# The band of softmax weights by column group, its zeroing on VectorE, and one scaling that may start three units sooner

## The chip, the cores and the metric

The kernel runs on one core of one Trainium2 chip. The metric is the time of one execution on the device in microseconds (us); of several runs the median is given. The engines are TensorE (PE in the profile, its weight loads PEld), VectorE (DVE), ScalarE (ACT), GpSimd (POOL) and SyncE (SP). SP and POOL issue nearly all DMAs here.

## The reference

Two branches work on the same input x of 2048 tokens by 1024. Branch a is an attention with 32 heads of 32 channels in which each token sees eight tokens: itself and those 2, 4, ... 14 before it. Branch b is a gated feed-forward layer with 3584 hidden channels. A sigmoid gate per token mixes the two.

```python
x = A_x
g = _sigmoid((x * gate_w).sum(-1, keepdims=True))
a = _A_ref(x, A_wqkv, A_wo)      # q, k, v; softmax over 8 keys at distance 0, 2, .. 14; times v; times wo
b = _B_ref(x, B_w_gate, B_w_up, B_w_down)   # (gelu(x @ w_gate) * (x @ w_up)) @ w_down
return g * a + (1 - g) * b
```

Inputs and result are bf16.

## The kernel before, in words

The big matrix products use a Strassen-like scheme of seven products in place of eight, so every group of weights and of activations is first combined by additions on VectorE. The tokens are worked on in two halves, s = 0 and 1, of 1024.

**Units.** The first 70% of the time is a list of units (class `Unit`, line 372). A unit is 28 products of 128x512 (line 381), about 6.05 us of TensorE, and goes through `p1`, `p5` and `p26`, while the unit before it finishes with `p73` and `p4`. TensorE's order per unit is: p1 of this unit, p73 of the one before, p5, the attention's slots, p26, and p4 of the one before. ScalarE copies partial sums between PSUM banks and evacuates them (lines 398, 403, 386 or 388, 410). VectorE adds two banks at once in line 417; the product of p4 overwrites one of these banks, so TensorE waits for line 417 there. The units are first one pair of the feed-forward layer, then q and k for both halves, then v, then the rest of gate and up. For the q and k units the weights are read with a step of eight columns (line 482).

**Background work on VectorE.** Everything else that VectorE does is a task: a generator that records some instructions and then yields their estimated cost in us. `bg(gen, prio, wake)` (line 448) puts a task in a list ordered by priority, the smallest first, and `wake` is the first unit in which it may run. At the end of each unit's recording `run_bg` (line 456) takes steps from the first awake task until a credit of some 4.7 us is used up. Each engine executes its instructions in the order in which they were recorded. So a task that is awake earlier, or has another cost, moves all others.

**The attention's second half.** The softmax weights of every head are written to DRAM (`w_d`, line 728). For each window of 114 tokens (`BQ`) and each half the kernel builds a band matrix: for 128 keys by 114 tokens by 32 heads, with the eight weights of a token on their diagonals and zero elsewhere. Its steps are these, and `pv_plan` (line 797) gives each a unit counted from the unit b in which the last softmax tasks allow it:

- `pv_init` (line 738, unit b): zeroes three band buffers `band` of 128 x 3648 bf16 and two staging tiles `ct` of 128 x 480, and stores the zeros to three DRAM copies `b_d`. All of it is on POOL.
- `pv_weights` (line 746, units b+2 and b+13): SP loads the weights from `w_d`.
- `pv_turn` (line 751): TensorE transposes two tiles of 128x128 (line 756), ScalarE copies them into `ct` (line 759), POOL writes `ct` into `b_d` with a row step that puts each weight on its diagonal (line 762).
- `pv_fetch` (line 764): two units later SP loads the nonzero parts of the band in three pieces (line 770), and the 128 rows of v (line 773).
- `pv_mm` (line 777): three units after that, 16 products per half of the heads (line 783). Each has a stationary operand of 32 columns of v and a moving operand of one head's band, 114 columns. The four heads c = 0 to 3 go to four groups of 32 output partitions, so that four products run beside each other. ScalarE evacuates them (line 786).

The band lies as [token][head], so the columns of one head's band are 32 elements, or 64 bytes, apart in SBUF.

**The results of gate and up** are multiplied by line 262, multiplied by 1 - g where they are among the last pairs (line 265), and stored to `h_d` by POOL (line 268). The tiles that hold them form a ring of five (`st_tile`, line 232).

**The end.** `run_last` and `down` (line 1107) multiply the hidden channels by w_down and the attention by wo, in one product whose left operand is loaded back from `h_d` and `o_d`. Those loaded blocks that were not multiplied by 1 - g before are scaled on VectorE by `scale_task` (line 950, its instruction is line 955). `pre_down_0` (line 990) loads the first eleven blocks of the operand A21 ten units before the end (n is the number of units) and makes a task of priority 6 of their scaling; it may run from unit n - 2. The other scalings have priorities 3, 7 and 8.

Of the kernel before, what the change touches and what calls it, by code (L numbers as in the profile page):

```python
# [10 lines left out]
BF16 = mybir.dt.bfloat16  # L11
F32 = mybir.dt.float32
AX = mybir.AxisListType
AP = bass.AP

P = 128
SC = 512
SUP = 2 * SC
NWIN = 8
DIL = 2  # L20
HALO = 16
AC = 256
NJ = 4
# [29 lines left out]
BQ = 114  # L53
BK = BQ + HALO - DIL
NSUB = 3
SQ = BQ // NSUB
R_BAND = (32, 39.125, 46.25)
# [3 lines left out]
R_CT = (72, 90)  # L61
# [7 lines left out]
def _win_ap(src: bass.AP, dims):  # L69
    return AP(src.tensor, src.offset, [list(src.ap[0])] + [list(d) for d in dims])  # L70
# [3 lines left out]
def kernel(  # L74
# [12 lines left out]
    nc = tc.nc  # L87
# [7 lines left out]
    NT = KT  # L95
# [12 lines left out]
    def reg(kb, n):  # L108
        o = int(kb * KB)
        return arena[:, o:o + n]  # L110

    def reg3(kb, a, b):
        return reg(kb, a * b).rearrange("p (a b) -> p a b", a=a)

    def reg4(kb, a, b, c):
        return reg(kb, a * b * c).rearrange("p (a b c) -> p a b c", a=a, b=b)
# [6 lines left out]
    def bank(i):  # L123
        return banks[:, i, :]
# [12 lines left out]
    PW = HALO + SUP + HALO  # L137
    w_d = [tc.dram_tile([32, NWIN, PW], BF16, name=f"w_d{s}") for s in range(2)]
    BC = BQ + 2 * (HALO - DIL)
    b_d = [tc.dram_tile([BK, BC, 32], BF16, name=f"b_d{k}") for k in range(3)]  # L140

    V = nc.vector
    TT = V.tensor_tensor

    with tc.manual_schedule(engines={mybir.EngineType.PE, mybir.EngineType.DVE, mybir.EngineType.Activation,
# [42 lines left out]
        for s in range(2):  # L188
            b0 = R_X[s]
            f = XF()  # L190
# [10 lines left out]
        def flat(a):  # L201
            return a.rearrange("p a b -> p (a b)")
# [245 lines left out]
        def bg(gen, prio, wake):  # L448
            t = Task(gen, prio, wake)
            tasks.append(t)  # L450
            tasks.sort(key=lambda t_: t_.prio)
            return t
# [33 lines left out]
        def add_unit(*a, **k):  # L486
            u = Unit(*a, **k)
            u.n = len(units)
            units.append(u)
            return u  # L490
# [31 lines left out]
        for s in range(2):  # L522
            for t in range(NT):
                u = add_unit(qk_forms(t), xf[s], "qkv", lambda s=s, t=t: qk_tile(s, t))
# [42 lines left out]
        for s in range(2):  # L567
            for t in range(4):
                u = add_unit(v_forms(), xf[s], "qkv", st_first if s + t == 0 else st_tile, rows=t)
# [5 lines left out]
        for i in range(NPAIR):  # L575
            n0 = len(units)
            w, sm = raw[i % 2], sums[i % 2]
# [11 lines left out]
        prod = [reg3(o, NWIN, AC) for o in pr_off]  # L589
        attn_all = reg3(R_ATTN, NBLK, SC)  # L590
        mask = reg3(R_MASK, NWIN, SJ)
        band = [reg3(o, BQ, 32) for o in R_BAND]
        NPT = SUP + HALO - DIL
        pt = [[reg(o, NPT) for o in r] for r in R_PT]
        o_all = reg3(R_OALL, NT, SUP)
        vw = [reg(o, D) for o in R_VW]
        ct = [reg3(o, 2 * NWIN - 1, 32) for o in R_CT]

        def mask_init():
            V.memset(mask, 0.0)  # L600
# [135 lines left out]
        rows = lambda i: min(BQ, SUP - BQ * i)  # L736

        def pv_init():
            for k in range(3):
                nc.gpsimd.memset(band[k], 0.0)  # L740
            for k in range(2):
                nc.gpsimd.memset(ct[k], 0.0)
            for k in range(3):
                nc.gpsimd.dma_start(out=b_d[k][:, HALO - DIL:HALO - DIL + BQ, :], in_=band[k])

        def pv_weights(s):
            for h in range(2):
# [3 lines left out]
        def pv_turn(g):  # L751
            s, i = wins[g]
            K = rows(i) + HALO - DIL
            ps = bank(7).bitcast(BF16)[:, 0:2 * P]
            for h in range(2):
                nc.tensor.transpose(out=ps[0:K, h * P:(h + 1) * P], in_=pt[s][h][:, BQ * i:BQ * i + K], identity=ident[:])
            c = ct[g % 2]
            for h in range(2):
                nc.scalar.copy(out=_win_ap(c[0:K, 0, 16 * h:16 * h + 1], [[2 * 32, NWIN], [1, 16]]),  # L759
                               in_=ps[0:K, h * P:(h + 1) * P].rearrange("k (w h) -> k w h", w=NWIN))  # L760
            d = b_d[g % 3]
            nc.gpsimd.dma_start(out=AP(d[:].tensor, d[:].offset, [[(BC + 1) * 32, K], [1, (2 * NWIN - 1) * 32]]), in_=flat(c[0:K]))  # L762

        def pv_fetch(g):
            s, i = wins[g]
            n_ = rows(i)
            for b in range(NSUB):
                qa, qz = SQ * b, min(SQ * (b + 1), n_)
                kz = qz + HALO - DIL
                nc.sync.dma_start(out=band[g % 3][qa:kz, qa:qz, :],  # L770
                                  in_=b_d[g % 3][qa:kz, qa + HALO - DIL:qz + HALO - DIL, :])
            r0 = HALO + s * SUP + BQ * i - (HALO - DIL)
            nc.sync.dma_start(out=vw[g % 3][0:n_ + HALO - DIL, :], in_=v_d[r0:r0 + n_ + HALO - DIL, :])

        def pv_mm(g, e, bk):
            s, i = wins[g]
            n_, q0 = rows(i), BQ * i
            K = n_ + HALO - DIL
            b = bank(bk)
            for t in range(4):  # L780
                for c in range(4):
                    h = 16 * e + 4 * t + c
                    nc.tensor.matmul(b[32 * c:32 * c + 32, t * BQ:t * BQ + n_], lhsT=vw[g % 3][0:K, 32 * h:32 * h + 32],  # L783
                                     rhs=_win_ap(band[g % 3][0:K, 0, h:h + 1], [[32, n_]]), start=True, stop=True,
                                     skip_group_check=True)
            nc.scalar.copy(out=o_all[:, 4 * e:4 * e + 4, q0:q0 + n_],
                           in_=b[:, 0:4 * BQ].rearrange("p (t q) -> p t q", t=4)[:, :, 0:n_])
            for c in range(2 * e):
                if q0 < (c + 1) * SC <= q0 + n_:
                    nc.gpsimd.dma_start(out=o_d[s][c][:], in_=o_all[:, :, c * SC:(c + 1) * SC])  # L790
# [3 lines left out]
        def pv_put(u, fn):  # L794
            pv_at.setdefault(u, []).append(fn)

        def pv_plan(b):
            pv_put(b, pv_init)
            pv_put(b + 2, lambda: pv_weights(0))
            pv_put(b + 13, lambda: pv_weights(1))  # L800
            for g in range(len(wins)):
                u = b + 9 + 3 * (g // 2)
                m0, m1, bk = (u + 1, u + 2, 6) if g % 2 else (u, u, 7)
                pv_put(m0, lambda g=g: pv_mm(g, 0, 6))
                pv_put(m1, lambda g=g, bk=bk: pv_mm(g, 1, bk))
                pv_put(u - 5 + g % 2, lambda g=g: pv_turn(g))
                pv_put(u - 3 + g % 2, lambda g=g: pv_fetch(g))
# [32 lines left out]
        for s in range(2):  # L840
            for t in range(NT):
                n_ = Q0 + NT * s + t
# [104 lines left out]
        def Bs(s):  # L947
            return {k: bufs[v] for k, v in plan[s].items()}

        def scale_task(b, s, c, ia, ib):  # L950
            t0 = s * SUP + c * SC
            om = omgrep[:, t0:t0 + SC].rearrange("p (o s) -> p o s", o=1)
            for i0 in range(ia, ib, 4):
                i1 = min(i0 + 4, ib)
                TT(out=b[:, i0:i1, :], in0=b[:, i0:i1, :], in1=om.to_broadcast([P, i1 - i0, SC]), op=ALU.mult)
                yield 0.05 + 0.273 * (i1 - i0)
# [31 lines left out]
        KX = int(R_P5A[0] - R_BUF[6])  # L988

        def pre_down_0(s):  # L990
            load_A(Bs(s)["A21"], s, 0, 1, 0, KX, False)
            bg(scale_task(Bs(s)["A21"], s, 1, 0, KX), 6, n - 2)

        def pre_down_2(s):
            pd["end"] = True
# [270 lines left out]
        n = len(units)  # L1266
# [82 lines left out]
```

## Time and profile before

| what | us |
|---|---|
| median of three runs (763.45 to 764.57) | 764.52 |
| the profiled execution | 762.28 |
| its span, first to last instruction | 760.5 |
| TensorE busy | 743.9 |
| VectorE busy | 532.3 |
| ScalarE busy | 354.3 |
| POOL busy | 165.1 |
| products with the band, line 783 | 34.2 |
| zeroing on POOL, lines 740 and 742 | 9.4 + 1.0 |
| products of the units, line 381 | 476.8 |

The granted clock of TensorE was 1.000 over the whole run. The band's products lie between 299.9 and 493.9 us, the zeroing between 236.0 and 246.3, the last units before 555. Matmuls overlap, so the busy time of a line is less than its count times the mean of one. A row of the timeline gives start, length, engine, line, operation, operands, shape and count, and in brackets how long the engine had been idle before it and who ended that.

### The profile page before, as it was taken

How to read it: one execution, taken by the hardware profiler on the slowest of the kernel's cores; microseconds unless marked ns; L12 is line 12 of the kernel's file. 1: busy time of each engine (PE TensorE's matmuls, PEld its weight loads, DVE VectorE, ACT ScalarE, POOL GpSimd, SP SyncE). 2: the span in 40 equal slices, each digit the busy share in tenths (PEclk: the TensorE clock that was granted, in tenths of full speed). 3: DMA queues.
4: the chain of work that ended last, by engine and by line, in shares of the span. 5: the costliest groups of instructions: out<-in, count | busy, mean ns of one | idle time of the engine just before them, and what ended most of it. 6: DMA issues, size and time to landing. Idle time of an engine off the chain costs nothing. (4 is left out here: it accounts for less than half of the span.)

```text
span 760.5 us, 12049 instructions
## 1 busy us (share of the span) xinstructions
PE 743.9 (98%) x4651; PEld 415.2 (55%) x4719; DVE 532.3 (70%) x562; ACT 354.3 (47%) x672; POOL 165.1 (22%) x271
## 2 busy tenths in 40 slices
PE   8999999999999999999999999999999999999998
PEld 4466566544444444444444444444445887658887
DVE  3699899999999443423333323335689999979997
ACT  4544445445556655565556555555413241132331
POOL 2233434343507522121211010000011001200011
PEclk9999999999999999999999999999999999999999
DMA  9986444394642977667665484475681589995961
GB/s 283 261 211 229 142 134 151 115 352 161 188 153 67 363 234 247 193 209 246 187 206 160 143 267 149 165 253 210 255 311 70 218 323 378 422 428 233 378 250 56
DMA packets 91118, 171.11 MB, mean 225 GB/s; under 512 B 20564, under 2 KB 62006, under 8 KB 86708
## 3 DMA queue, kind: packets, MB, share of 16 engines
q1 hardware_dynamic: 72676, 109.39, 42.8%
q0 software_dynamic: 17664, 53.34, 20.4%
q10 hardware_dynamic: 720, 7.60, 2.6%
q8 instruction: 37, 0.61, 0.3%
q14 instruction: 21, 0.17, 0.1%
HBM read 116.10 MB, written 59.18 MB: 230 GB/s over the span
## 5 line engine op out<-in xcount | busy, mean ns | idle before, releaser
L381 PE MATMUL banks<-arena 128*128 128x512 bf16 x2125 | 476.8, 379 | 8.2 <-DVE arena L417 2.8
L381 PEld LDWEIGHTS <-arena 128*128 128x128 bf16 x2184 | 231.2, 107 | 244.3 <-issue 16.3
L417 DVE TENSOR_TENSOR arena<-banks,arena 128x1024 bf16<-128x1024 f32 x78 | 95.4, 1223 | 188.7 <-PE banks L381 99.8
L1083 PE MATMUL banks<-arena 128*128 128x256 bf16 x1260 | 138.8, 273 | 0.6 <-DVE arena L1049 0.6
L1083 PEld LDWEIGHTS <-arena 128*128 128x128 bf16 x1260 | 123.1, 98 | 16.6 <-issue 1.3
L403 ACT COPY arena<-banks 128x512 f32<-128x512 f32 x78 | 46.1, 591 | 130.4 <-PE banks L381 130.4
L388 ACT CAST arena<-banks 128x512 bf16<-128x512 f32 x102 | 59.6, 585 | 44.7 <-PE banks L381 42.2
L612 DVE TENSOR_TENSOR arena<-arena 128x2048 bf16<-128x2048 bf16 x64 | 74.6, 1218 | 0.1
L1116 PE MATMUL banks<-arena 128*128 128x512 bf16 x281 | 62.4, 379 | 0.4
L410 ACT COPY banks<-banks 128x512 f32<-128x512 f32 x78 | 44.5, 571 | 23.7 <-PE banks L381 19.2
L1041 DVE TENSOR_TENSOR arena<-arena 128x2304 bf16<-128x2304 bf16 x40 | 53.2, 1351 | 0.5
L268 POOL DMA_DIRECT2D h_d<-arena x28 | 20.7, 738 | 143.2 <-DVE arena L262 100.8
L398 ACT COPY banks<-banks 128x512 f32<-128x512 f32 x78 | 44.9, 576 | 13.6 <-PE banks L381 12.0
L1088 ACT COPY banks<-banks 128x256 f32<-128x256 f32 x60 | 21.4, 356 | 61.8 <-PE banks L1083 61.6
L1116 PEld LDWEIGHTS <-arena 128*128 128x128 bf16 x288 | 28.2, 98 | 33.5
L331 DVE TENSOR_TENSOR arena<-arena 128x1024 bf16<-128x1024 bf16 x60 | 38.7, 685 | 5.1 <-DMA arena<-in_B_w_up_dram 4.6
L964 DVE TENSOR_TENSOR arena<-arena 128x2048 bf16<-128x2048 bf16 (+1 forms) x40 | 41.7, 1109 | 0.0
L386 ACT ACTIVATE arena<-banks 128x512 bf16<-128x512 f32 x54 | 32.2, 597 | 15.7 <-PE banks L381 15.2
L1049 DVE TENSOR_TENSOR arena<-arena 128x2304 bf16<-128x2304 bf16 x28 | 37.6, 1350 | 0.3
L262 DVE TENSOR_TENSOR arena<-arena 128x2048 bf16<-128x2048 bf16 x28 | 34.1, 1216 | 4.2 <-ACT arena L388 2.8
L783 PE MATMUL banks<-arena 128*32 128x114 bf16 (+1 forms) x576 | 34.2, 381 | 0.0
L762 POOL DMA_DIRECT2D b_d<-arena x18 | 10.3, 572 | 108.3 <-ACT arena L759 98.2
(102 smaller groups left out, 507.7 us busy)
## 6 DMA issues: line engine op xcount, KB each, us to landing
arena<-t_d SPq DMA_DIRECT2D x8, 2304.0 KB
h_d<-arena POOLq DMA_DIRECT2D x28, 512.0 KB, 5.0
arena<-w_c SPq DMA_DIRECT2D x12, 1152.0 KB
t_d<-arena POOLq DMA_DIRECT2D x36, 256.0 KB, 4.0
arena<-h_d SPq DMA_DIRECT2D x6, 1536.0 KB
arena<-in_B_w_gate_dram SPq DMA_DIRECT2D x15, 512.0 KB
arena<-in_B_w_up_dram SPq DMA_DIRECT2D x15, 512.0 KB
arena<-in_B_w_down_dram SPq DMA_DIRECT2D x28, 256.0 KB
```

Source lines behind the costliest of these rows:

```text
L331: TT(out=o_, in0=a, in1=b_, op=op)
L381: self.pe = nc.tensor.matmul(ps, lhsT=l, rhs=r, start=(start and kt == 0), stop=(kt == HK - 1), skip_group_check=not start)
L388: nc.scalar.copy(out=o_, in_=i_)
L398: nc.scalar.copy(out=self.Y, in_=self.X)
L403: nc.scalar.copy(out=self.p5s, in_=self.V)
L410: nc.scalar.copy(out=self.Z, in_=self.Y)
L417: TT(out=self.T[:, :, c2s], in0=pair, in1=self.p5s.rearrange("p (o n) -> p o n", o=1).to_broadcast([P, 2, SC]), op=ALU.add)
L612: TT(out=dst, in0=q.rearrange("p (o s) -> p o s", o=1).to_broadcast([P, NWIN, AC]), in1=_win_ap(k, [[-DIL, NWIN], [1, AC]]), op=ALU.mult)
L964: TT(out=f(o_), in0=f(a), in1=f(b), op=op)
L1041: TT(out=o_, in0=a, in1=b_, op=op)
L1083: nc.tensor.matmul(c(i, h, j), lhsT=l[:, kt, j * P:(j + 1) * P], rhs=r[:, kt, :], start=False, stop=(kt == KH - 1), skip_group_check=True)
L1116: nc.tensor.matmul(ps, lhsT=L[:, i, j * P:(j + 1) * P], rhs=R[:, i, :], start=(start and q == 0), stop=(q == NK - 1), skip_group_check=not ...
```

## The change

There are three edits.

1. The band lies as [c][token][8 heads], in SBUF (`band`), in the staging tiles (`ct`) and in DRAM (`b_d`). Head 16e + 4t + c is element 4e + t of group c. The columns of one head are 8 elements, or 16 bytes, apart, and the four products that run beside each other read from four blocks that are 114 x 8 elements apart. Each row of the DMAs breaks into four pieces. ScalarE's copies in line 759 read as before and write single elements 240 bytes apart, where they wrote 16 side by side.
2. The zeroing is on VectorE. `pv_init` becomes a task of priority 0 that is awake in unit b; it yields 1.2 after each band buffer, and POOL stores the zeros of each buffer behind that step.
3. The scaling of A21 may run from unit n - 5 in place of n - 2.

```diff
--- before.py
+++ after.py
@@ -137,7 +137,8 @@
     PW = HALO + SUP + HALO
     w_d = [tc.dram_tile([32, NWIN, PW], BF16, name=f"w_d{s}") for s in range(2)]
     BC = BQ + 2 * (HALO - DIL)
-    b_d = [tc.dram_tile([BK, BC, 32], BF16, name=f"b_d{k}") for k in range(3)]
+    b_d = [tc.dram_tile([NJ, BK, BC, NT], BF16, name=f"b_d{k}") for k in range(3)]
+    assert NT * NJ == 32
 
     V = nc.vector
     TT = V.tensor_tensor
@@ -589,12 +590,12 @@
         prod = [reg3(o, NWIN, AC) for o in pr_off]
         attn_all = reg3(R_ATTN, NBLK, SC)
         mask = reg3(R_MASK, NWIN, SJ)
-        band = [reg3(o, BQ, 32) for o in R_BAND]
+        band = [reg4(o, NJ, BQ, NT) for o in R_BAND]
         NPT = SUP + HALO - DIL
         pt = [[reg(o, NPT) for o in r] for r in R_PT]
         o_all = reg3(R_OALL, NT, SUP)
         vw = [reg(o, D) for o in R_VW]
-        ct = [reg3(o, 2 * NWIN - 1, 32) for o in R_CT]
+        ct = [reg4(o, NJ, 2 * NWIN - 1, NT) for o in R_CT]
 
         def mask_init():
             V.memset(mask, 0.0)
@@ -736,12 +737,13 @@
         rows = lambda i: min(BQ, SUP - BQ * i)
 
         def pv_init():
+            for k in range(2):
+                V.memset(ct[k], 0.0)
             for k in range(3):
-                nc.gpsimd.memset(band[k], 0.0)
-            for k in range(2):
-                nc.gpsimd.memset(ct[k], 0.0)
-            for k in range(3):
-                nc.gpsimd.dma_start(out=b_d[k][:, HALO - DIL:HALO - DIL + BQ, :], in_=band[k])
+                V.memset(band[k], 0.0)
+                yield 1.2
+                nc.gpsimd.dma_start(out=b_d[k][:, :, HALO - DIL:HALO - DIL + BQ, :].rearrange("c k q t -> k c (q t)"),
+                                    in_=band[k].rearrange("k c q t -> k c (q t)"))
 
         def pv_weights(s):
             for h in range(2):
@@ -756,10 +758,11 @@
                 nc.tensor.transpose(out=ps[0:K, h * P:(h + 1) * P], in_=pt[s][h][:, BQ * i:BQ * i + K], identity=ident[:])
             c = ct[g % 2]
             for h in range(2):
-                nc.scalar.copy(out=_win_ap(c[0:K, 0, 16 * h:16 * h + 1], [[2 * 32, NWIN], [1, 16]]),
-                               in_=ps[0:K, h * P:(h + 1) * P].rearrange("k (w h) -> k w h", w=NWIN))
+                nc.scalar.copy(out=_win_ap(c[0:K, 0, 0, 4 * h:4 * h + 1], [[2 * NT, NWIN], [1, 4], [(2 * NWIN - 1) * NT, NJ]]),
+                               in_=ps[0:K, h * P:(h + 1) * P].rearrange("k (w t c) -> k w t c", w=NWIN, t=4))
             d = b_d[g % 3]
-            nc.gpsimd.dma_start(out=AP(d[:].tensor, d[:].offset, [[(BC + 1) * 32, K], [1, (2 * NWIN - 1) * 32]]), in_=flat(c[0:K]))
+            nc.gpsimd.dma_start(out=AP(d[:].tensor, d[:].offset, [[(BC + 1) * NT, K], [BK * BC * NT, NJ], [1, (2 * NWIN - 1) * NT]]),
+                                in_=c[0:K].rearrange("k c u t -> k c (u t)"))
 
         def pv_fetch(g):
             s, i = wins[g]
@@ -767,8 +770,9 @@
             for b in range(NSUB):
                 qa, qz = SQ * b, min(SQ * (b + 1), n_)
                 kz = qz + HALO - DIL
-                nc.sync.dma_start(out=band[g % 3][qa:kz, qa:qz, :],
-                                  in_=b_d[g % 3][qa:kz, qa + HALO - DIL:qz + HALO - DIL, :])
+                nc.sync.dma_start(out=band[g % 3][qa:kz, :, qa:qz, :].rearrange("k c q t -> k c (q t)"),
+                                  in_=b_d[g % 3][:, qa:kz, qa + HALO - DIL:qz + HALO - DIL, :]
+                                  .rearrange("c k q t -> k c (q t)"))
             r0 = HALO + s * SUP + BQ * i - (HALO - DIL)
             nc.sync.dma_start(out=vw[g % 3][0:n_ + HALO - DIL, :], in_=v_d[r0:r0 + n_ + HALO - DIL, :])
 
@@ -781,7 +785,7 @@
                 for c in range(4):
                     h = 16 * e + 4 * t + c
                     nc.tensor.matmul(b[32 * c:32 * c + 32, t * BQ:t * BQ + n_], lhsT=vw[g % 3][0:K, 32 * h:32 * h + 32],
-                                     rhs=_win_ap(band[g % 3][0:K, 0, h:h + 1], [[32, n_]]), start=True, stop=True,
+                                     rhs=band[g % 3][0:K, c, 0:n_, 4 * e + t], start=True, stop=True,
                                      skip_group_check=True)
             nc.scalar.copy(out=o_all[:, 4 * e:4 * e + 4, q0:q0 + n_],
                            in_=b[:, 0:4 * BQ].rearrange("p (t q) -> p t q", t=4)[:, :, 0:n_])
@@ -795,7 +799,7 @@
             pv_at.setdefault(u, []).append(fn)
 
         def pv_plan(b):
-            pv_put(b, pv_init)
+            bg(pv_init(), 0, b)
             pv_put(b + 2, lambda: pv_weights(0))
             pv_put(b + 13, lambda: pv_weights(1))
             for g in range(len(wins)):
@@ -989,7 +993,7 @@
 
         def pre_down_0(s):
             load_A(Bs(s)["A21"], s, 0, 1, 0, KX, False)
-            bg(scale_task(Bs(s)["A21"], s, 1, 0, KX), 6, n - 2)
+            bg(scale_task(Bs(s)["A21"], s, 1, 0, KX), 6, n - 5)
 
         def pre_down_2(s):
             pd["end"] = True
```

## The prediction

> **What bounds the kernel now.** I read the page's busy line first, then the list of who waited for whom on TensorE, then single stretches of the timeline, and last the groups of weight loads.
>
> ```profile
> PE 743.9 (98%) x4651; PEld 415.2 (55%) x4719; DVE 532.3 (70%) x562; ACT 354.3 (47%) x672; POOL 165.1 (22%) x271
> ```
>
> TensorE is busy for 98% of the 760.5 us span. So a change can help in two ways only: it shortens TensorE's own work, or it removes one of TensorE's few waits. These are the long ones that the change can touch (time, count, longest, in us):
>
> ```profile
> PE banks L381 <- DVE arena L417: 2.8, 2, 2.3
> PE banks L381 <- ACT arena L388: 1.2, 1, 1.2
> ...
> PE banks L756 <- DMA arena<-w_d: 1.1, 1, 1.1
> ```
>
> TensorE's own work that is touched is the 576 products of line 783, whose moving operand is the band. They run as waves of four: c = 0 to 3 write four groups of 32 output partitions at once. Three stretches of the timeline price a wave (start, length, engine):
>
> ```profile
> 299.95 1.86 PE L783 MATMUL banks<-arena 128*32 128x114 bf16 x32
> ...
> 62.90 1.48 PE L617 MATMUL banks<-arena,ones_r 128*32 128x512 bf16 x24
> ...
> 4.49 1.07 PE L221 MATMUL banks<-ident,arena 128*128 128x128 bf16 x16 [0.56 <-DMA arena<-in_A_x_dram]
> ```
>
> The first line holds eight waves. Less one product's 0.385 us, seven steps take 1.475, so 0.211 us a wave, for 114 columns that lie 64 bytes apart. The second holds six waves of 512 columns that lie side by side: (1.48 - 0.38) / 5 = 0.22 us. The third, a single stream of 128 columns side by side, steps by (1.07 - 0.22) / 15 = 0.057 us. So the band's wide step costs about 0.154 us a wave, or 0.34 ns for each of its 4 x 114 = 456 elements.
>
> No moving operand in this trace steps by 16 bytes, as the new band does. A stationary one does: the weights of the q and k units take every eighth column (line 482). The first line is 60 to 140 us, inside those units; the second is 160 to 230 us, the same instruction with columns side by side (the two numbers behind the bar are busy us and mean ns):
>
> ```profile
> L381 PEld LDWEIGHTS <-arena 128*128 128x128 bf16 x322 | 45.7, 144 | 25.5 <-issue 3.1
> ...
> L381 PEld LDWEIGHTS <-arena 128*128 128x128 bf16 x311 | 30.2, 98 | 37.9 <-issue 1.9
> ```
>
> The step of 16 bytes costs 46 ns for 128 elements: 0.36 ns each, the same as 64 bytes cost the band.
>
> The second place is the stretch around the zeroing:
>
> ```profile
> 236.03 9.40 POOL L740 MEMSET arena<- 128x3648 bf16 x3
> ...
> 242.27 1.22 DVE L262 TENSOR_TENSOR arena<-arena 128x2048 bf16<-128x2048 bf16 x1
> ...
> 247.75 0.86 POOL L268 DMA_DIRECT2D h_d<-arena  x1
> ...
> 248.10 1.22 DVE L417 TENSOR_TENSOR arena<-banks,arena 128x1024 bf16<-128x1024 f32 x1
> ...
> 257.39 0.58 ACT L388 CAST arena<-banks 128x512 bf16<-128x512 f32 x1 [2.54 <-DMA h_d<-arena]
> ...
> 258.02 3.61 PE L381 MATMUL banks<-arena 128*128 128x512 bf16 x15 [1.22 <-ACT arena L388]
> ...
> 269.24 0.23 PE L756 MATMUL banks<-ident,arena 128*128 128x128 bf16 x1 [1.13 <-DMA arena<-w_d]
> ```
>
> VectorE finishes a block of h at 243.5, but its store leaves only at 247.75, because POOL is still zeroing and issuing the zeros' stores. The store lands late, ScalarE waits 2.54 us for the tile it frees, and TensorE 1.22 us for ScalarE. At 269.24 TensorE waits again, for the first softmax weights from w_d.
>
> The third is the last units:
>
> ```profile
> 546.78 1.23 DVE L265 TENSOR_TENSOR arena<-arena,omgrep 128x2048 bf16<-128x2048 bf16 x1
> 547.92 3.22 DVE L955 TENSOR_TENSOR arena<-arena,omgrep 128x2048 bf16<-128x2048 bf16 x3
> 548.36 0.58 ACT L403 COPY arena<-banks 128x512 f32<-128x512 f32 x1 [1.97 <-PE banks L381]
> ...
> 551.06 1.22 DVE L417 TENSOR_TENSOR arena<-banks,arena 128x1024 bf16<-128x1024 f32 x1
> 552.34 2.75 PE L381 MATMUL banks<-arena 128*128 128x512 bf16 x11 [2.29 <-DVE arena L417]
> ```
>
> The three scalings of line 955 are those of A21. They stand ahead of line 417, the addition that frees TensorE's bank, and TensorE waits 2.29 us, its longest wait.
>
> **The change part by part.**
>
> *The band's step, 64 to 16 bytes.* 144 waves. Bounds: if 16 bytes cost as little as side by side, a wave falls to 0.057 us and 144 x 0.154 = 22.2 us go. If each element costs what the weight load's cost, 0.36 ns, a wave is 0.057 + 456 x 0.00036 = 0.221, and 1.4 us are added. I take 0: the weight load is the only row with this very step, and it pays per element what the band pays now. [...]
>
> *ScalarE's copies (line 759).* 36 of 0.272 us now write single elements 240 bytes apart instead of runs of 16. Between nothing and a doubling: up to 0.54 us a unit on an engine that is 47% busy. The evacuation behind them (line 388) waited 0.19 to 0.38 us for TensorE there, so it could be 0.35 us late; X has two banks by then, so its next use is a unit (6 us) away. 0; without the second bank it would be those 0.35 us in 18 units.
>
> *The DMAs.* Counts and queues stay; each row breaks in four: 960 bytes into 240 (18 writes), 2432 into 608 (54 fetches), 7296 into 1824 (3 zero stores). In the trace's packet records a packet of 2432 bytes takes 98 ns, one of 512 takes 27 and one of 1024 takes 46, so four of 608 some 124: 2800 rows x 26 ns / 16 engines = 4.6 us spread over 180 us. A write issued at 270.57 is fetched at 278.7 and lands in 2.3 us (6.2 at most); the fetch serves a product at 299.95. 0, as long as those 6 and 20 us of cover stand. POOL's own issue (0.57 us) can rise to the 0.74 of line 268, which has 512 pieces: 3 us on an engine 22% busy.
>
> *Zeroing on VectorE.* POOL loses 9.4 + 1.0 us. VectorE gets five word memsets. Its rows of 256 and 64 words take 272 and 112 ns, so 0.83 ns a word and 0.06 fixed: 3 x 1.58 + 2 x 0.26 = 5.3 us. In the built order they stand behind line 262 and ahead of line 701, with line 417 next and line 703 and the transforms of line 911 behind it. So: 243.4 + 5.3 + 0.7 = 249.4 for a line 417 that started at 248.10, done at 250.6. TensorE needs it at 249.9 (ScalarE's line 410 there, at 249.94, ends on the product before). Cost 0.7 us (0 to 1.5). The last softmax block moves two units later; its weights are read 13 units after the plan, so that is covered, and its table loads merely change units. What goes: the h store now stands ahead of the zeros' stores on POOL and leaves at about 243.6, so the 1.22 us at 258.02 go, and with them most of 0.22 us at 261.85.
>
> What is late next is the wait for w_d at 269.24. If that landing stays, TensorE merely waits there longer and the stretch gives 0. The page's slices say that DMA moved 67 GB/s from 228 to 247 us and 363 from 247 to 266; h's 0.5 MB and the first 0.9 MB of zeros now fall into the idle end of the first, which takes some 1 MB, or up to 2.5 us, off what the load of w_d competes with. Then the stretch gives 1.22 + 0.22 + 1.13 - 0.7 = 1.9. Between 0 and 1.9 I take 1.3, since the queue was idle until 245.
>
> *The scaling three units sooner.* Its three multiplications (3.3 us) move from behind 547.92 to the unit at 527, behind line 265 there, in the built order. There they end at 530.3; line 417 waited idle 2.42 us until 529.42, so it is 0.9 late and done at 531.5. TensorE's next need is at 532.0, after the 12 products that follow. Cover 0.5 us. A21's loads left SP at 483 to 494, 30 us earlier. At the old place line 417 starts at 548.0, done at 549.2, before the 550.05 at which TensorE stopped. So 2.29 us go. VectorE then works without a gap from 555 to 591, but that block begins with the last line 417, which waits for TensorE and moves along; I keep 2.2.
>
> **Sum:** 0 - 1.3 - 2.2 = -3.5 us. The profiled execution took 762.28 us (span 760.5), 2.24 under the median of 764.52. So 758.8 there, a span of 757.0, and 761.0 as a median. What this kernel's measurement can tell from no change is about 0.2%, 1.5 us.
>
> **The rivals.**
>
> *The step of 16 bytes is free.* For it: the wave's 0.211 us is almost all step. Against it: the weight loads. Full price 761.0 - 22.2 = 738.8; if only every second element pays, 761.0 - 11.1 = 749.9. [...] Chance 0.22.
>
> *The waits come back elsewhere.* w_d lands as late as now, and the 2.2 us run into VectorE's forms (line 1049, for which TensorE waits 0.6 us already) or into loads of h by POOL that hang on a store and not on TensorE. Then 764 to 765.5. Chance 0.10.
>
> *Slower: the zeros choke the loads.* POOL's stores of t_d already wait for the b_d stores (1.6 us), and its next issues come 2 us apart. With 1536 pieces in place of 384, starting no sooner than VectorE has zeroed, the loads of w_d and of the up weights (line 331 waits 4.6 us for those) can land y later. The stretch then costs y, the total is y - 2.2, and it is slower from y = 3.7. At 7 us: 769.3. Against it: the bytes are the same and begin earlier. Chance 0.07.
>
> [...] Now the four products of a wave read neighbours 2 bytes apart, then 1824 apart. If they share fetches now, a wave grows; from 35 ns a wave (144 x 35 = 5.0) it is slower, and at 60 ns the time is 769.6. Against it: the weight load's elements lie apart too and pay no more. Chance 0.05.
>
> **How the numbers follow.** The forecast has 0.56, and its own range is 758.5 to 763: sum of the ends 0 to -1.9, +1.4 for the waves and 0.9 more for the zeroing. Faster: the 0.22 and nearly all of the 0.56 (0.53), so 0.75. Same: 0.10 and the rest, 0.13. Slower: 0.12. The range runs from 742 to 765.5: it leaves out the two slower rivals (0.12) and the deeper third of the free step (0.08).
>
> **What would show it.** Right: the line 783 group of 32 stays near 1.86 us; no wait of ScalarE's line 388 for h_d near 257; the store of h leaves before 245; TensorE's wait for line 417 falls from 2.8 to under 1.2 us; line 955 stands near 527; two memset groups on VectorE sum to about 5.3 us. Wrong: a group of 32 at 1.0 us or under (the free step) or over 2.2; a wait for w_d of over 4 us; a wait for line 417 of over 1.5 us at 250 or at 532.

## The result

The changed kernel took 758.79 us (median of four executions, 758.31 to 759.09), the kernel before 764.55 us (763.45 to 765.0) beside it. The ratio is 0.9926, with a 95% interval of 0.9909 to 0.9943: 5.8 us faster. The forecast was 761.0 us. The profiled execution took 758.93 us with a span of 757.2 (forecast: 758.8 and 757.0). So two differences have to be explained, not one: 3.35 us between the two profiled executions, and 5.8 us between the medians.

In the changed kernel's code the lines stand a little lower: 417 is now 418, 388 is 389, 268 is 269, 756 is 758, 759 is 761, 265 is 266, 783 is 787 and 955 is 959. The zeroing is in lines 741 and 743, its stores in line 745.

First two lines of the changed kernel's page: the busy line, and the band products from the list of groups.

```profile
PE 748.1 (99%) x4719; PEld 416.4 (55%) x4719; DVE 537.5 (71%) x567; ACT 365.0 (48%) x672; POOL 159.8 (21%) x266
...
L787 PE MATMUL banks<-arena 128*32 128x114 bf16 (+1 forms) x576 | 34.3, 381 | 0.0
```

The band products are busy for 34.3 us, against 34.2 before. The step of 16 bytes brought nothing. These are the longest of TensorE's waits in the changed kernel:

```profile
PE banks L382 <- DVE arena L418: 2.1, 2, 1.5
PE banks L160 <- DVE arena L157: 1.2, 1, 1.2
PE banks L1087 <- DVE arena L1053: 0.6, 1, 0.6
```

The waits for an evacuation (1.2 us) and for w_d (1.1 us) are gone. Of the two waits for the addition of two banks, the one of 2.3 us in the last units is gone, and one of 1.5 us has come. The timeline of the changed kernel shows where:

```profile
244.29 0.73 POOL L269 DMA_DIRECT2D h_d<-arena  x1 [7.65 <-DVE arena L263]
...
244.84 1.58 DVE L743 MEMSET arena<- 128x1824 uint32 x1 [0.33 <-issue]
...
246.74 1.58 DVE L743 MEMSET arena<- 128x1824 uint32 x1 [0.33 <-issue]
...
248.65 1.58 DVE L743 MEMSET arena<- 128x1824 uint32 x1 [0.33 <-issue]
...
250.69 1.21 DVE L418 TENSOR_TENSOR arena<-banks,arena 128x1024 bf16<-128x1024 f32 x1
...
251.95 16.56 PE L382 MATMUL banks<-arena 128*128 128x512 bf16 x76 [1.54 <-DVE arena L418]
...
268.35 0.28 PE L758 MATMUL banks<-ident,arena 128*128 128x128 bf16 x2
```

The store of h leaves at 244.3, ahead of the zeros. The two transposes at 268.35 follow each other without a wait, where the second waited 1.13 us before. And in the last units:

```profile
526.21 3.22 DVE L959 TENSOR_TENSOR arena<-arena,omgrep 128x2048 bf16<-128x2048 bf16 x3
529.35 1.22 DVE L418 TENSOR_TENSOR arena<-banks,arena 128x1024 bf16<-128x1024 f32 x1
...
546.06 1.23 DVE L266 TENSOR_TENSOR arena<-arena,omgrep 128x2048 bf16<-128x2048 bf16 x1
547.21 1.22 DVE L418 TENSOR_TENSOR arena<-banks,arena 128x1024 bf16<-128x1024 f32 x1
```

The scaling stands at 526 and the addition at 547.2 starts as soon as line 266 is done, 3.9 us earlier than before.

Where the 3.35 us lie is read from single instructions that both profiled executions have (start in us; the third column of numbers is the difference, from unrounded times, and the last is what the stretch ending there contributed):

| instruction | before | after | difference | in this stretch |
|---|---|---|---|---|
| 33rd addition of two banks | 241.13 | 241.64 | +0.51 | +0.51 |
| second transpose of the first window | 269.24 | 268.41 | -0.83 | -1.34 |
| last band product | 493.45 | 492.73 | -0.73 | +0.10 |
| first product of the end | 554.92 | 551.76 | -3.17 | -2.44 |
| end of the span | 760.50 | 757.15 | -3.35 | -0.18 |

The first half microsecond has arisen by the first product of a unit (25.01 us before, 25.52 after), ahead of anything that the change touches. The zeroing's stretch gave 1.34 us and the last units 2.44.

### The profile page after: what moved, and what is told of

It is laid out like the page before. It is cut to its first block, busy times and chain, and to the rows that moved or that the text cites. A ratio compares the mean times of both kernels' runs of the same rounds, so it can differ in the third digit from the quotient of the medians.

```text
span 757.2 us, 12107 instructions
## 1 busy us (share of the span) xinstructions
PE 748.1 (99%) x4719; PEld 416.4 (55%) x4719; DVE 537.5 (71%) x567; ACT 365.0 (48%) x672; POOL 159.8 (21%) x266
## 5 line engine op out<-in xcount | busy, mean ns | idle before, releaser
L389 ACT CAST arena<-banks 128x512 bf16<-128x512 f32 x102 | 62.8, 615 | 39.3 <-PE banks L382 38.5
L387 ACT ACTIVATE arena<-banks 128x512 bf16<-128x512 f32 x54 | 35.3, 653 | 12.4 <-PE banks L382 12.2
L764 POOL DMA_DIRECT2D b_d<-arena x18 | 14.3, 795 | 110.7 <-ACT arena L761 96.9
L787 PE MATMUL banks<-arena 128*32 128x114 bf16 (+1 forms) x576 | 34.3, 381 | 0.0
```

Of the source, the lines that this page charges most:

```text
L389: nc.scalar.copy(out=o_, in_=i_)
```

## The experiments

Three questions were open: whether the parts are worth what they seem, why the medians moved 2.4 us more than the profiled executions, and what the step of the moving operand costs.

### One part at a time, and the kernel before once more

The layout alone (the changed kernel with these two parts undone):

```diff
-            bg(pv_init(), 0, b)
+            pv_put(b, pv_init)
...
-            for k in range(2):
-                V.memset(ct[k], 0.0)
-            for k in range(3):
-                V.memset(band[k], 0.0)
-                yield 1.2
+            for k in range(3):
+                nc.gpsimd.memset(band[k], 0.0)
+            for k in range(2):
+                nc.gpsimd.memset(ct[k], 0.0)
...
-            bg(scale_task(Bs(s)["A21"], s, 1, 0, KX), 6, n - 5)
+            bg(scale_task(Bs(s)["A21"], s, 1, 0, KX), 6, n - 2)
```

> Only the band's layout is changed; zeroing stays on POOL and the scaling at n - 2. Theory (the step of 16 bytes costs what 64 bytes cost): the 32 band products that stand together stay near 1.86 us, line 783's group stays at 34.2 us, the long waits of the kernel before (2.3 us for the addition of two banks in the last units, about 1.2 us for an evacuation behind a late store) stay, and the time is within 1.5 us of the kernel before, the dearer copies of ScalarE (0.90 us in place of 0.27 us) included. Rival (the layout is what brings the 2.4 us by which the medians moved more, 5.8, than the two profiled executions, 3.35): 2 us faster or more.

Measured: 764.9 us against 763.7 (ratio 1.0018, 1.0008 to 1.0027). It is within the theory's 1.5 us and on the slower side, so the rival falls. This difference of medians mixes executions in which TensorE's clock dropped, as is shown below, with others: it did in 10 of these 12 and in 12 of the 23 of the kernel before. Between the two profiled executions, neither of which has a drop, the zeroing's stretch is 1.4 us longer. The band products are where they were. What it costs lies in the zeroing's stretch, by the list of TensorE's waits in this kernel:

```profile
PE banks L382 <- ACT arena L389: 2.1, 1, 2.1
PE banks L758 <- DMA arena<-w_d: 1.6, 1, 1.6
```

Those were 1.2 and 1.1 us in the kernel before. Here POOL's three zero stores, each with four times the pieces, take 0.82 us each to issue, against 0.65. The store of h behind them leaves at 248.6 in place of 247.75, and the evacuation that waits for its landing starts at 258.5 in place of 257.4.

The zeroing alone:

```diff
+            for k in range(2):
+                V.memset(ct[k], 0.0)
             for k in range(3):
-                nc.gpsimd.memset(band[k], 0.0)
-            for k in range(2):
-                nc.gpsimd.memset(ct[k], 0.0)
-            for k in range(3):
+                V.memset(band[k], 0.0)
+                yield 1.2
...
-            pv_put(b, pv_init)
+            bg(pv_init(), 0, b)
```

> Only the zeroing moves to VectorE. Theory: the late store of h goes, a wait of some 1.5 us for the addition of two banks comes, the wait for the first softmax weights goes or shrinks; 1.3 us faster (0 to 2). Rival (the medians' further 2.4 us lie here, because the kernel before loses more at these waits in most executions than in its profiled one): 3 us faster or more.

Measured: 762.22 us against 763.7 (ratio 0.998, 0.9971 to 0.999), 1.5 us faster: near the theory's 1.3. Up to the second transpose it gains 1.35 us on the kernel before. So the further 2.4 us do not lie here. This difference of medians, too, mixes executions with and without the drop, 9 of 12 with it here. Like with like it is 1.65 us without the drop (760.62 against 762.27) and 2.06 with it (762.24 against 764.30).

The scaling alone (`n - 2` becomes `n - 5`, nothing else):

> Only the scaling of A21 may start at n - 5. Theory: the 2.3 us wait in the last units goes and nothing takes its place: 2.2 us faster. Rival (some of the end is set by loads that do not move along): 1 us or less.

Measured: 759.91 us against 763.7 (ratio 0.9959, 0.9944 to 0.9974), 3.8 us faster. In the profiled execution it gains 2.44 us from 541 us to the first product of the end, the theory's 2.2. But the medians move 1.4 us more. The further microseconds hang on this part.

The kernel before, unchanged:

> The kernel before, unchanged, profiled once more. Theory: the stretch from 241 to 270 us, with its waits for a late store and for the first softmax weights, takes longer or shorter from one execution to the next by 1 us or more, since both waits end with DMAs that compete; the rest repeats within 0.5 us. Rival: every stretch repeats within 0.3 us, and the executions differ before the first or after the last instruction.

Measured: one execution of 763.94 us, with a span of 762.1, against 762.28 and 760.5 in the profile that was first shown. Theory and rival both fall. The stretch from 241 to 270 us repeated within 0.15 us. The last units did not: from the addition at 551 us to the first product of the end it took 5.55 us, where it was 3.86. The stretch by stretch view says why (length of the stretch, busy us of PE, PEld, DVE, ACT and POOL with the count of instructions, then the granted clock, the DMA share and GB/s). First the profile shown at the start, then this one:

```profile
550.00:553.00 3.00, 0.71 (x5) 0.30 (x4) 2.28 (x3) 0.57 (x1) 0.00 (x0) 1.00 0.75 312
553.00:556.00 3.00, 2.95 (x14) 1.35 (x14) 0.82 (x1) 1.54 (x2) 1.05 (x2) 1.00 0.02 7
```

```profile
550.00:553.00 3.00, 0.76 (x3) 0.36 (x3) 2.19 (x3) 0.57 (x1) 0.00 (x0) 0.91 0.70 289
553.00:556.00 3.00, 3.00 (x9) 1.01 (x8) 0.00 (x0) 1.54 (x2) 1.59 (x3) 0.52 0.06 20
```

In the second execution TensorE's granted clock was 0.52 from 553 to 556 us: right behind its wait of 2.3 us it ran at half speed, and had 9 products there where it had had 14. The clock's own records in the trace have one stretch at a half, 3.413 us long. So the wait cost 2.3 us by itself, and in this execution 1.7 us more.

The same records say why one execution pays and another does not. Within each trace all changes of the clock, the first rise to full speed among them, lie on a grid of 3.413 us, whose place against the kernel differs from one execution to the next. In the profile shown at the start full speed begins 4.48 us into the span and lasts 757.76 us, 222 intervals; in the changed kernel's it begins at 6.92 us and lasts 750.93 us, 220 intervals. The grid's intervals around the wait are these, two of the profile shown at the start and two of this one:

```profile
547.20:550.61 3.41, 2.85 (x14) 1.18 (x12) 3.41 (x4) 1.17 (x2) 0.71 (x1) 1.00 1.02 424
550.61:554.02 3.41, 1.63 (x7) 0.78 (x8) 1.67 (x2) 1.20 (x3) 0.00 (x0) 1.00 0.49 202
```

```profile
549.03:552.44 3.41, 1.12 (x6) 0.39 (x4) 3.16 (x4) 0.75 (x2) 0.12 (x1) 1.00 0.90 369
552.44:555.86 3.42, 3.42 (x9) 1.17 (x8) 0.00 (x0) 1.95 (x3) 1.45 (x3) 0.50 0.05 16
```

In the first execution a grid line splits the wait of 2.29 us, TensorE is idle for 1.78 us at most in one interval, and the clock stays. In the second the whole wait falls into one interval, and the next one runs at a half. The other profiles with this wait agree: split (1.76 us at most) and no drop with the layout alone, 2.24 us in one interval and a drop with the zeroing alone and in the first of the two probes below.

The mean clocks of the executions without a profile agree. Of the 23 of the kernel before in this job, 12 had a mean clock of 0.998 or less and took 763.7 to 764.95 us; the other 11 had 0.999 or more, eight of them between 761.95 and 762.47 and three near 763.2. A halving for 3.4 us of 760 lowers the mean by 0.0022, which is that 0.998. The zeroing alone, which leaves the 2.3 us wait, splits in the same way: 760.6 to 761.2 us at 1.000 (three executions), 762.05 to 762.5 at 0.997 or 0.998 (nine). The scaling alone, which removes the wait, has 0.999 or 1.000 in all six. In the two later jobs the kernel before has 0.998 or less in 6 of 12 and in 6 of 9 executions, and in each of the three jobs every execution at 0.998 or less took longer than every one above.

### What the step of the moving operand costs

Two kernels let the products read the band at other steps, window by window; the products then use other elements of it, so their output is not the attention's. The first is the kernel before with

```diff
-                                     rhs=_win_ap(band[g % 3][0:K, 0, h:h + 1], [[32, n_]]), start=True, stop=True,
+                                     rhs=_win_ap(flat(band[g % 3][0:K])[:, h:h + 1], [[(32, 16, 8, 4, 2, 1)[g % 6], n_]]), start=True, stop=True,
```

> The kernel before, in which the moving operand of the band products steps by 64, 32, 16, 8, 4 and 2 bytes in windows 0 to 5 in turn, and so on; the products then read other elements of the band, so their values are not the attention's. Theory (an element alone on its 16 bytes pays 0.34 ns, two or more share): a wave of four takes 0.21 us at 64, 32 and 16 bytes, about 0.13 at 8 bytes, under 0.10 at 4 and 2. Rival (the price depends on the step in another way, and only the four streams' distance or a larger unit of reading matters): 16 or 32 bytes are already cheaper than 64, or only 2 bytes is cheap. About 288 waves in 12 windows... in each of the six steps 24 waves; the whole saves up to 8 us, less if the clock of TensorE drops.

and the second the changed kernel, with its four streams in four blocks:

```diff
-                                     rhs=band[g % 3][0:K, c, 0:n_, 4 * e + t], start=True, stop=True,
+                                     rhs=_win_ap(band[g % 3][0:K, c, 0, 4 * e + t:4 * e + t + 1], [[(8, 4, 2, 1, 8, 4)[g % 6], n_]]), start=True, stop=True,
```

> The changed kernel, with the moving operand stepping by 16, 8, 4, 2, 16 and 8 bytes in windows 0 to 5 in turn, its four streams in four blocks 1824 bytes apart; the products read other elements of the band, so their values are not the attention's. Theory: the distance of the streams does not matter, so each step costs what it costs in the other probe, 0.21 us a wave at 16 bytes. Rival (streams that lie 2 bytes apart share fetches): the steps below 16 bytes cost more here than there.

Each probe was executed once. The median distance between the starts of two waves inside a group of 16 products, in us:

| step, bytes | streams 2 bytes apart | streams 1824 bytes apart |
|---|---|---|
| 64 | 0.199 | |
| 32 | 0.207 | |
| 16 | 0.203 | 0.203 |
| 8 | 0.104 | 0.104 |
| 4 | 0.053 | 0.057 |
| 2 | 0.052 | 0.051 |

The timeline of the first probe (start, length) shows the same. Its first row is a group of 32 products at 16 bytes, the second a group of 16 at 8 bytes, the third a group of 32 at 4 bytes:

```profile
324.07 1.82 PE L783 MATMUL banks<-arena 128*32 128x114 bf16 x32
...
331.97 0.60 PE L783 MATMUL banks<-arena 128*32 128x114 bf16 x16
...
345.54 0.62 PE L783 MATMUL banks<-arena 128*32 128x114 bf16 x32
```

From 64 down to 16 bytes nothing changes (0.199 to 0.207 us); at 8 bytes the price halves (0.104); at 4 it is at the floor that columns side by side have (0.053 and 0.057 against 0.052 and 0.051). The runs show these prices, not what lies behind them. How far apart the four streams lie makes no difference at 16 and 8 bytes and at most 0.004 us below, so both of the rivals that set a price on it fall. The theory was right but for the 8 bytes, which cost 0.104 where 0.13 was expected. The whole of the first probe took 756.2 us and of the second 747.1.

### Versions that could be better

The old layout with the other two parts, and with costs for the zeroing's steps near the measured ones (shown against the zeroing of the changed kernel):

```diff
                 V.memset(ct[k], 0.0)
+            yield 0.6
             for k in range(3):
                 V.memset(band[k], 0.0)
-                yield 1.2
+                yield 2.0
```

> The band's old layout, with the zeroing on VectorE and the scaling at n - 5, and with costs near the measured ones for the zeroing's steps: 0.6 for the two staging tiles and 2.0 for each band buffer in place of 1.2, so that one of the three band buffers falls into the next unit. Theory: the wait of 1.5 us for the addition of two banks near 250 us falls below 0.3 us, ScalarE's copies are back at 0.27 us, and the time is 1 to 1.5 us below the changed kernel, 757.5. Rival (VectorE's later work in the next units brings the wait back, or the zeros' stores come so late that the first softmax weights are waited for): no faster than the changed kernel.

Measured: 757.71 us against 763.94 (ratio 0.9921, 0.9903 to 0.9939). One of the band buffers now falls into the next unit, behind an addition of two banks that starts at 248.6, and the wait of 1.5 us is gone. What is left of the waits for it sums to 1.3 us, 0.8 at the longest, so the theory's 0.3 was too good. The time is near the 757.5 expected, but the changed kernel's own median in this job lies 2.6 us above it, not 1 to 1.5; between the two profiled executions it is 1.0 (757.34 and 758.34). Beside it the changed kernel, unchanged:

> The changed kernel, unchanged, beside the others. Theory (the kernel before loses a further 1.6 us in most executions, when TensorE's clock is halved for 3.4 us behind the 2.3 us wait of the last units, and the changed kernel, which has no wait of that length, never does): all executions show a clock of 0.999 or more and lie within 1 us of each other, near 758.5, while those of the kernel before lie in two groups some 1.7 to 2 us apart. Rival (the two groups have another cause): the changed kernel has two groups too.

Measured: 760.3 us (758.34 to 761.29) against 763.94, ratio 0.9952 (0.9934 to 0.997). All seven executions have a mean clock of 0.999 or 1.000, as expected, and the kernel before had 0.997 or 0.998 in six of its twelve. So the rival, two groups here too, falls. But they do not lie within 1 us of each other, as was expected; they spread over 3 us without any drop of the clock. The profiled ones of all kernels place their first product of a unit between 24.8 and 26.8 us, so up to 2 us can arise in the first loads. Whether that is the spread here was not settled. Nor does the 95% interval here reach the 0.9926 of the first result: the medians of the changed kernel in its two jobs differ by 1.5 us.

The kernel before with the zeroing and the scaling of the change, so that it differs from the changed kernel by the layout alone (the memsets on VectorE, as in the zeroing alone, are left out here):

```diff
-            pv_put(b, pv_init)
+            bg(pv_init(), 0, b)
...
-            bg(scale_task(Bs(s)["A21"], s, 1, 0, KX), 6, n - 2)
+            bg(scale_task(Bs(s)["A21"], s, 1, 0, KX), 6, n - 5)
```

> The changed kernel with the old layout of the band, costs of the zeroing's steps as in the change (1.2). It differs from the changed kernel by the layout alone. Theory (the layout costs nothing once the zeros' stores have left the stretch from 241 to 270 us): within 0.7 us of the changed kernel, and some 1.5 us above the kernel with true costs, since TensorE's wait near 250 us is back. Rival (the layout's pieces and copies cost what they cost alone, 1.2 us): 1.2 us or more below the changed kernel.

Measured: 758.95 us (757.86 to 759.08) against 764.52, ratio 0.9926 (0.9914 to 0.9938). That is the changed kernel's own ratio in the first result. The changed kernel did not run in this job, and its medians in two other jobs differ by 1.5 us; the two profiled executions decide, with spans of 757.12 and 757.15 us and starts within 0.11 us of each other at each row of the table above. So the layout is worth nothing in the change, and its own cost of 1.2 us disappears when the zeros' stores no longer stand ahead of h.

Last, a step at which the band is cheap. With four heads in a block the columns are 8 bytes apart, with two 4 bytes. The version with four is shown against the changed kernel; the band, the staging tiles and ScalarE's copies follow the same blocks, and the zeroing's steps have the costs 0.6 and 2.0:

```diff
-    b_d = [tc.dram_tile([NJ, BK, BC, NT], BF16, name=f"b_d{k}") for k in range(3)]
+    HT, HG = 4, 32 // 4
+    b_d = [tc.dram_tile([HG, BK, BC, HT], BF16, name=f"b_d{k}") for k in range(3)]
...
-                                     rhs=band[g % 3][0:K, c, 0:n_, 4 * e + t], start=True, stop=True,
+                                     rhs=band[g % 3][0:K, 4 * e + c, 0:n_, t], start=True, stop=True,
```

> The band in eight blocks of four heads, so that a head's columns are 8 bytes apart, with the zeroing on VectorE at costs near the measured ones and the scaling at n - 5. Theory: a wave of four products takes 0.104 us, as the probe had for 8 bytes, so 144 waves save 14 us against the kernel without a new layout (757.7): about 743.5, less what the smaller DMA pieces (304 and 120 bytes) cost, which stay hidden. Rival (the pieces, twice as many as in the changed kernel, or ScalarE's scattered copies come to lie on the path): 748 or more, with waits for b_d or w_d on TensorE.

Measured: 742.38 us (742.0 to 743.64) against 764.52, ratio 0.9716 (0.9702 to 0.973). This is the best of all versions, and its median is 16 us below the changed kernel's. The costs of the zeroing's steps have a part in that; against the old layout with the same costs, 757.71, it is 15.3 us, near the expected 14. Its first group of 32 and its band products:

```profile
297.52 1.01 PE L788 MATMUL banks<-arena 128*32 128x114 bf16 x32
```

```profile
L788 PE MATMUL banks<-arena 128*32 128x114 bf16 x512 | 17.4, 280 | 0.0
...
L788 PE MATMUL banks<-arena 126*32 126x112 bf16 x64 | 2.1, 278 | 0.0
```

The group of 32 takes 1.01 us, where it was 1.86, and the products are busy for 19.5 us where it was 34.2. The smaller pieces stay hidden: TensorE waits for no band.

With two heads in a block:

> The band in sixteen blocks of two heads, columns 4 bytes apart, zeroing and scaling as in the kernel beside it. Theory: a wave takes 0.053 us, so 144 x 0.148 = 21 us are saved: about 736.5, if DMA pieces of 152 and 60 bytes stay hidden. Rival (four times the changed kernel's pieces: POOL's issue and the landing of a 60-byte write grow past the 8 us before its fetch): 741 or more, with waits on TensorE for the band.

Measured: 777.8 us against 764.52, ratio 1.0179 (1.0164 to 1.0193). Its waves are as cheap as expected, 0.055 us. But the list of its waits shows the rival, and more than it said. First TensorE's waits, then one of VectorE's, then the page's line on DMA packets:

```profile
PE banks L382 <- DVE arena L418: 12.8, 4, 5.2
PE banks L759 <- DMA arena<-w_d: 10.3, 2, 7.1
PE banks L788 <- DMA arena<-v_d: 8.0, 3, 3.9
```

```profile
DVE arena L332 <- DMA arena<-in_B_w_up_dram: 48.2, 5, 15.4
```

```profile
DMA packets 133546, 171.11 MB, mean 220 GB/s; under 512 B 65440, under 2 KB 106956, under 8 KB 129136
```

The kernel before moves 91118 packets, 20564 of them under 512 bytes; this one 133546 and 65440, for the same 171 MB. SP needs 1.67 us (median, 7.6 at most) to issue one fetch of the band, where it needed 0.37. SP issues the up weights and the rows of v behind these fetches, so they come late; VectorE waits 48 us for the up weights, and with it the addition of two banks for which TensorE waits. The wait at the band products themselves, the third line's 8.0 us, is for the rows of v and is the smaller part of it.

The waits of these three lines sum to 31 us, and the time is 41 us above the expected 736.5. The clock accounts for most of the rest: the mean clock was 0.980, and the trace has six stretches at a half, 30.7 us in all, each beginning during one of these waits or within 1.2 us of its end. TensorE had work for 22.4 us of them, which at half speed costs some 11 us.

## Why the prediction was right, and where it was not

*What bounds the kernel:* right that TensorE's work and its waits do. A third thing that moved the time was not in it: TensorE's clock, at a half for 3.413 us behind a wait of 2.3 us.

*The band's step:* right, 0 against +0.10 us measured over the whole phase. The weight loads with the same step had given the price (0.36 ns an element, against the band's 0.34), and the probes confirm it: 16, 32 and 64 bytes are one price (0.203, 0.207 and 0.199 us a wave). The rival of a free step falls, and so does that of four streams that lie apart (0.203 us at 16 bytes both 2 and 1824 bytes apart).

*ScalarE's copies:* the bound was wrong, and it cost nothing. A doubling was the far end; the copies went from 0.272 to 0.90 us, 3.3 times as long:

```profile
L761 ACT COPY arena<-banks 128x128 bf16<-128x128 bf16 (+1 forms) x36 | 23.3, 901 | 0.0
```

The cover named there, a second bank for X and an engine half idle, held: without the layout the span of the profiled execution is the same within 0.03 us.

*The DMAs:* right. Writes of the band land in 3.5 us (2.3 before), and POOL's issue takes 0.80 us (0.57 before, 0.74 forecast at most); the covers of 6 and 20 us hold. At four times as many pieces again they are gone, as the kernel with two heads shows.

*Zeroing on VectorE:* the sum was right, 1.34 us against 1.3, by luck: two terms missed and cancelled. The memsets took the 1.58 and 0.26 us that were worked out, but VectorE stood idle for 0.33 us ahead of each of the three large ones, so that TensorE waited 1.54 us and not 0.7. On the other side the wait for w_d went altogether, of which only a part was counted. With the measured waits the terms give 1.22 + 0.22 + 1.13 - 1.54 = 1.03 us; the other 0.3 us were not traced. The reason given for w_d, more bytes in the idle end of the queue, is not what the traces show: from 244 to 248 us DMA moved 172 GB/s, 175 before. The stores of the zeros did not begin earlier, either; they left at 246.7, 248.6 and 250.5 us where they had left at 246.1, 246.7 and 247.2. What did change is that h's store left 3.5 us earlier, and that the last softmax block, with its four stores of weights between 260.7 and 263.7 us, moved out of this stretch. Which of them brought w_d in time was not tried. The rival of zeros that choke the loads fell, but not for the reason argued against it.

*The scaling:* right in its mechanism. In the profiled executions the last units gave 2.44 us, forecast 2.2, and none of it came back later, so the rival in which the waits come back elsewhere falls.

*From the profiled execution to the median:* this is the step that failed. The forecast carried the difference of 2.24 us between the profiled execution and the median over to the changed kernel, as if it belonged to the measuring. By the later executions most of it belonged to the wait that the scaling removes: the profiled execution was one of those in which the clock was not halved behind the wait, and in the job with 23 executions the two kinds have medians 2.0 us apart (762.27 and 764.30). The clocks of the first three timed executions are not on record, and in one job the changed kernel's median lay 2.0 us above its profiled execution without any drop, so how the 2.24 us divide is not shown. So the term for the scaling was sized at 2.2 us, and was worth 2.4 and about 1.7 more in each execution with a halved clock, 3.8 us between the medians when it was changed alone. In the first result the changed kernel's median lies 0.1 us under its profiled execution, not 2.2 above.

The sum for the profiled execution, 758.8, met 758.93. The median was forecast 2.2 us too high. It lies in the range given for the likeliest case, 758.5 to 763, but that range does not follow from the ends named for it: 764.52 - 2.2 less 1.9 is 760.4, and 764.52 - 2.2 with 1.4 and 0.9 more is 764.6. The measured 758.79 lies below both, so that it fell into the range is luck.

## What to carry to other kernels

A wait of TensorE of 2.3 us cost 1.7 us more here where it fell into one interval of the clock's grid, so compare the profiled execution's mean clock with those of the other executions before a difference between them is carried along. To price an access pattern that the trace lacks, look for any other instruction with the same step, also a weight load: it gave the right price here, where a step of 16 bytes saves nothing. When one big layout change hides small edits, undo it alone: here the two small edits were the whole gain, and the layout one step further was worth 15 us.

## What the runs showed of the hardware that was not expected

- A wait of 2.3 us was enough for TensorE's clock to be halved for 3.41 us, in about half of the executions of the kernel before (12 of 23, 6 of 12, 6 of 9), at a cost of 1.7 us. It depended on where the wait fell: 2.24 us of idle time within one interval of the 3.413 us grid halved the clock, 1.78 us did not.
- A moving operand read by four products side by side costs 1.8 ns a column at steps of 64, 32 and 16 bytes (0.203 us for 114 columns), 0.9 at 8 bytes and 0.45 at 4 and 2.
- ScalarE's copies of 128 columns out of PSUM take 0.90 us when each element goes 240 bytes from the last, against 0.27 in runs of 32 bytes.
- VectorE stood idle for 0.33 us ahead of each memset of 1824 words, with nothing in the profile that it waited for, also in the version in which one of them stood in another unit. What that is was not tried.
- 832 pieces of 152 bytes made SP's issue of one fetch 1.67 us long, against 0.37 us for 52 pieces; with 416 pieces of 304 bytes it was 0.44.
